# Sliding-window attention and a SMELU layer on one core: masks on VectorE, a new order of early loads and first-batch sessions, output quarters eight slots behind

## The chip, the cores and the metric

The kernel runs on one core of a Trainium2 chip. The metric is device time in microseconds for one execution; lower is better. The engines are TensorE (PE, with its weight loads as PEld), VectorE (DVE), ScalarE (ACT), GpSimd (POOL) and SyncE (SP, which only issues DMAs here).

## The reference

Eight batches of eight heads, 576 positions, head size 64. Attention looks at most 32 positions to each side. Its result, 4608 tokens by 512, goes through two weight matrices with a piecewise activation between them.

```python
scores = scale * np.matmul(q, k.transpose(0, 1, 3, 2))
mask = np.abs(pos[:, None] - pos[None, :]) <= window        # window = 32
attn = softmax(np.where(mask, scores, -1e9)); attn_out = np.matmul(attn, v)
x = attn_out.transpose(0, 2, 1, 3).reshape(B * S, H * D)    # 4608 x 512
h = x @ w_in                                                # 512 x 2048
g = np.where(h >= 1, h, np.where(h <= -1, 0.0, (h + 1) ** 2 / 4))
return g @ w_out                                            # 2048 x 512
```

## The kernel before, in words

All matmuls are in bf16. The order of the work on each engine is written out by hand (`manual_schedule`): an engine runs its instructions in the order in which the program issues them, and semaphores order engines against each other.

**The slots.** After a start-up part the main loop (L395) counts slots `a`. A slot works on token block t = a // 8 (256 tokens) and on f = a % 8 (256 of the 2048 hidden features). It issues eight matmuls of hp (L415, weights w_in, 256 columns each), on ScalarE rr = relu(0.5 h + 0.5) (L419), on VectorE mx = max(h, rr) (L422) and gT = min(rr, 1) * mx (L423). That product is the activation. The hp tiles come from two PSUM banks (pool ps_h); in slots 2, 3, 6, 7, 10, 11 they come from the output pool ps_o instead (L409). Of 144 slots, those whose predecessor issued a GpSimd mask (list `masked`, L392) write the max back into hp rather than into a tile of its own in SBUF (L421).

**Output.** From slot 14 on (LAG = 14) each slot also issues four matmuls with w_out (L438). Sixteen make one tile of 128 tokens by 512, in one of two banks of ps_o. ScalarE then copies it to osb (L442), of which there are three, and SyncE stores it. After the last hidden slot, 14 slots of output matmuls are left.

**Attention sessions.** A batch has five score sessions and five sum sessions. The table `ev` says which slot issues which (L368 to L381). A score session (L198; `scores8`, L226, for the last 96 positions) computes blocks of scores with 64 by 64 matmuls into a tile of two banks, applies exp on ScalarE to pt (L222, L240), and masks. In slots below PEM = 28 (`eng` is None, L397) TensorE adds a mask matrix to the scores ahead of the exp (`add_mask`, L191). From slot 28 on GpSimd multiplies pt by a mask of zeros and ones (L224, L242). A sum session (L246) multiplies pt with v and with ones, and its `end` computes 1 / sum on ScalarE as exp(-ln(sum)) (L280, L281). VectorE's product with it, which writes xT (L286, L289), is put off to the beginning of the next slot (`flush`, L404). A token block's hidden slots need the xT of all sums over its tokens.

**q and k.** For batches 0 to 2 they are loaded in halves (`load_long`), and TensorE transposes them in slots listed in L382 (`tpose`, L169). Two copies of each go to ScalarE before slot 15, and after that one to ScalarE and one to VectorE. Batches 3 to 7 are loaded whole (`load_nat`) and transposed by DMA from SyncE's queue.

**Queues.** All loads but the first four pieces of q are issued by GpSimd, in program order, on one queue; the tile framework lets eight be under way. The early ones stand in L116 to L155: q and k of batch 0's first half, v of batch 0, four pieces of w_in with 256 columns, then q and k of the second half mixed with the six larger pieces of w_in (`mix` puts one large load ahead of two small ones), batch 1's first half mixed with its v, w_out in quarters, and so on. Later loads are issued in slots fixed in L386 to L389; GpSimd's masks stand in the same queue.

Of the kernel before, what the change touches and what calls it, by code (L numbers as in the profile page):

```python
# [8 lines left out]
FP = mybir.dt.float32  # L9
# [6 lines left out]
def kernel(  # L16
# [19 lines left out]
    nc = tc.nc  # L36
# [67 lines left out]
    def load_w_in(c0, c1, h):  # L104
        nc.gpsimd.dma_start(out=w_in[64 * h:64 * h + 64, :, c0:c1],
                            in_=moe_w_in.rearrange("(h y d) f -> h d y f", h=2, d=64)[h][:, :, c0:c1])
# [25 lines left out]
    V.memset(ones, 1.0)  # L132
    for t in qTs:
        V.memset(t[:, 0:PAD], 0.0)
    for c in range(0, 512, 256):
        for h in range(2):
            load_w_in(c, c + 256, h)

    def mix(small, large):

        for n in range(0, max(len(small), 2 * len(large)), 2):
            for fn, *x in large[n // 2:n // 2 + 1] + small[n:n + 2]:
                fn(*x)
# [1 line left out]
    def halves(b, half):  # L145
        return [(load_long, b, half, t, y) for t in range(2) for y in range(NY)]

    mix(halves(0, 1), [(load_w_in, c, c + 512, h) for c in (512, 1024, 1536) for h in range(2)])
    mix(halves(1, 0), [(load_v, 1, n) for n in range(4)])
    load_w_out(0)  # L150
    load_w_out(1)
    mix(halves(1, 1), [(load_w_out, 2), (load_w_out, 3)])
    mix(halves(2, 0), [(load_v, 2, n) for n in range(4)])
    for fn, *x in halves(2, 1):
        fn(*x)  # L155


    kT = {}
# [29 lines left out]

    pt, pt8 = {}, {}

    def add_mask(ps, n, w):  # L191
        for a in range(2):
            for h in range(2):
                nc.tensor.matmul(ps[HD[a], h, :n * w].rearrange("p (n j) -> p n j", n=n), ident[HD[h], HD[h]],
                                 bias[HD[h], :w].rearrange("p (n j) -> p n j", n=1).to_broadcast([64, n, w]),
                                 start=True, stop=False, skip_group_check=True)

    def scores(b, ys, pars, cs, eng, pool=ps_s):  # L198

        if b not in pt:  # L200
            pt[b] = ptp.tile([128, 2, 2, 2, 512], BF, name="pt")
        ps = two_banks(pool)
        n = 0
        if eng is None:
            cols = (ys[1] - ys[0]) * (pars[1] - pars[0]) * (cs[1] - cs[0])
            add_mask(ps, cols, 128)
        for y1 in range(*ys):
            for par in range(*pars):
                for c2 in range(*cs):
                    c = 2 * c2 + par  # L210
                    for a in range(2):
                        for h in range(2):
                            s0 = S * (y1 + 2 * a) + 64 * c
                            nc.tensor.matmul(ps[HD[a], h, 128 * n:128 * n + 128], kT[b][HD[h], s0:s0 + 64],  # L214
                                             qTs[b % 3][HD[h], PAD + s0 - 32:PAD + s0 + 96],
                                             start=eng is not None, stop=True, skip_group_check=True)
                    n += 1
        p = pt[b][:, :, ys[0]:ys[1], pars[0]:pars[1], 128 * cs[0]:128 * cs[1]]
        m = 2 if n > cs[1] - cs[0] else 1
        p = p[:, :, ys[0] - ys[0]] if ys[1] - ys[0] == 1 else p[:, :, :, 0]  # L220
        like = "p h (y j) -> p h y j"
        A.activation(p, ps[:, :, :128 * n].rearrange(like, y=m), AF.Exp, scale=D ** -0.5)  # L222
        if eng is not None:
            eng.tensor_mul(p, p, mask4[:, :256 * n].rearrange("p (h j) -> p h j", h=2).rearrange(like, y=m))  # L224

    def scores8(b, eng, pool=ps_s):  # L226

        p = pt8[b] = ptp.tile([128, 2, 2, TAIL], BF, name="pt8")
        ps = two_banks(pool)
        if eng is None:  # L230
            add_mask(ps, 2, TAIL)
        for y1 in range(2):
            for a in range(2):
                for h in range(2):
                    s0 = S * (y1 + 2 * a) + MAIN
                    nc.tensor.matmul(ps[HD[a], h, TAIL * y1:TAIL * y1 + TAIL], kT[b][HD[h], s0 + 32:s0 + TAIL],
                                     qTs[b % 3][HD[h], PAD + s0:PAD + s0 + TAIL],
                                     start=eng is not None, stop=True, skip_group_check=True)
        p = p.rearrange("p h y j -> p h (y j)")
        A.activation(p, ps[:, :, :2 * TAIL], AF.Exp, scale=D ** -0.5)  # L240
        if eng is not None:
            eng.tensor_mul(p, p, mask8.rearrange("p (h j) -> p h j", h=2))  # L242

    muls = []

# [102 lines left out]

    NB = NT // TB
    NF = DFF // 256
    LAG = 14
    PEM = 28
    ev, tps = {}, {}

    def at(a, *todo):
# [7 lines left out]
                yield (sums, b, y1, lo, hi), (scores, b, (y1, y1 + 1), (0, 2), (2 * k, 2 * k + 2))  # L365
        yield (sums, b, 0, MAIN, S), (scores8, b)

    at(4, (scores, 0, (0, 1), (0, 2), (2, 4)), (scores8, 0, ps_n))  # L368
    at(5, (sums, 0, 0, TB, MAIN), (scores, 0, (1, 2), (0, 2), (2, 4)))
    at(6, (sums, 0, 1, TB, MAIN, ps_s), (sums, 0, 0, MAIN, S))  # L370
    seq = [x for b in range(1, B) for x in steps(b, 224)]
    at(12, seq[0][0])
    at(13, (*seq[1][0], ps_s))
    for n, a in enumerate((20, 22, 25, 27)):
        at(a, seq[2 + n][0])
    for n, a in enumerate((10, 11, 19, 20, 21, 26, 27)):
        at(a, seq[n][1])
    sl = [30, 32, 35, 39, 42, 45, 49, 52, 56, 59, 62, 65, 69, 73, 77, 81, 84, 88, 92]
    sl += [96, 99, 103, 106, 110, 113, 116, 120, 124, 128]
    for n, a in enumerate(sl):  # L380
        at(a, seq[6 + n][0], seq[7 + n][1] if n < len(sl) - 1 else None)  # L381
    for b, half, *a in ((0, 1, 1, 3), (1, 0, 8, 9), (1, 1, 17, 18), (2, 0, 23, 24), (2, 1, 28, 29)):  # L382
        for t in range(2):
            tps[a[t]] = [(b, 2 * half + part, t) for part in range(2)]
    loads, xps = {}, {}
    for b in range(LONG, B):  # L386
# [2 lines left out]
            loads.setdefault(a + t, []).append((b, t))  # L389
        for t in range(2):  # L390
            xps.setdefault(a + 9 + 2 * t, []).append((b, t))
    masked = [a for a in ev if a >= PEM and any(x[0] is not sums for x in ev[a])]  # L392

    gT = {}
    for a in range(NF * NB + LAG):  # L395
        t, f = divmod(a, NF)
        eng = None if a < PEM else P  # L397
        for b, x in loads.get(a, []):
            if x < 2:
                load_nat(b, x)  # L400
            else:
                for n in range(4):
                    load_v(b, n)
        flush()  # L404
        if t < NB:
            if f == 0:
                gT[t] = gtp.tile([128, 2 * NF, TB], BF, name="gT", tag="gT")
            r0 = TB * t % RING
            if a < LAG and a % 4 > 1:  # L409
                hp = ps_o.tile([128, 2, TB], FP, name="hp", tag="op")  # L410
            else:
                hp = ps_h.tile([128, 2, TB], FP, name="hp", tag="hp")
            for j in range(2):
                for n, kk in enumerate((0, 2, 1, 3)):
                    nc.tensor.matmul(hp[:, j], w_in[:, kk, 256 * f + 128 * j:256 * f + 128 * j + 128],  # L415
                                     xT[:, kk, r0:r0 + TB], start=n == 0, stop=n == 3)

            rr = ewp.tile([128, 2, TB], FP, name="rr")
            A.activation(rr, hp, AF.Relu, scale=0.5, bias=0.5)  # L419

            mx = hp if a - 1 in masked else ewp.tile([128, 2, TB], FP, name="mx")  # L421
            V.tensor_max(mx, hp, rr)  # L422
            V.scalar_tensor_tensor(gT[t][:, 2 * f:2 * f + 2], rr, 1.0, mx, op0=ALU.min, op1=ALU.mult)  # L423
        ends = []
        for fn, *x in ev.get(a, []):
            if fn is sums:
                ends.append(sums(*x))
            else:
                pool = (x.pop(),) if x[-1] in (ps_s, ps_n) else ()
                fn(*x, eng, *pool)  # L430
        for end in ends:
            end()
        if a >= LAG:
            for x in range(4 * (a - LAG), 4 * (a - LAG) + 4):
                tt, ff = divmod(x, 2 * NF)
                if ff == 0:
                    op = ps_o.tile([128, DM], FP, name="op", tag="op")
                nc.tensor.matmul(op, gT[tt // 2][:, ff, 128 * (tt % 2):128 * (tt % 2) + 128], w_out[:, ff],  # L438
                                 start=ff == 0, stop=ff == 2 * NF - 1)
                if ff == 2 * NF - 1:  # L440
                    osb = osp.tile([128, DM], FP, name="osb")
                    A.copy(osb, op)  # L442
                    nc.sync.dma_start(out=out[128 * tt:128 * tt + 128, :], in_=osb)
        if a in tps:
            copies = [tpose(b, n, t, (A.copy, V.tensor_copy)[i if a > LAG else 0], tp1((ps_s, ps_n)[i]))
                      for i, (b, n, t) in enumerate(tps[a])]
            for x in copies:
                x()
        for x in xps.get(a, []):
            xpose(*x)  # L450
# [30 lines left out]
```

The softmax here doesn't subtract the row's maximum and nothing guards it: scores larger than these inputs give would overflow.

## Time and profile before

| | us |
|---|---|
| median of 10 runs | 328.06 |
| lowest and highest | 327.46, 329.72 |
| profiled execution, its time | 327.81 |
| profiled execution, its span | 325.9 |

The page of the profile gives shares over the whole span. TensorE's matmul records overlap in time, since their ends are modelled, so the distance from one start to the next tells the pace. The costliest groups, mean duration of one instruction:

| group | count | mean, ns |
|---|---|---|
| L415 hidden matmul, 256 columns | 1152 | 275 (a record) |
| L438 output matmul, 512 columns | 576 | 380 (a record) |
| L419 ScalarE rr | 144 | 595 |
| L422 VectorE max into mx, into hp | 116, 28 | 690, 692 |
| L423 VectorE gT from mx, from hp | 116, 28 | 746, 687 |
| L224 GpSimd mask of 1024, L242 of 384 | 22, 6 | 2192, 911 |
| L222 ScalarE exp | 32 full | 1023 |
| L280, L281 Ln and Exp of 512 | 16, 16 | 593, 630 |

Row 2 of the page cuts the span into 40 slices of 8.15 us. The table of stretches, shown below in rows, gives: the stretch, then for PE, PEld, DVE, ACT and POOL the busy time with the number of instructions, then granted clock, DMA share and GB/s.

### The profile page before, as it was taken

The numbers are of one execution on the slowest core, as the hardware profiler recorded it, in microseconds if no ns is written. First come the engines' busy times: TensorE is split into PE (matmuls) and PEld (weight loads), VectorE is DVE, ScalarE is ACT, GpSimd is POOL, SyncE is SP. The second block draws the span as 40 slices with busy tenths as digits, with TensorE's granted clock in tenths as the row PEclk, the third lists the DMA queues.
The fourth block names the chain that finished last, engine by engine and source line by source line (L and its number), as shares of the span: only waits on it lengthen the run. The fifth ranks groups of instructions, "written<-read, shape, count | busy, mean of one in ns | idle before, by whom it ended". The sixth has DMA issues, their size and how long they took to land.

```text
span 325.9 us, 8581 instructions
## 1 busy us (share of the span) xinstructions
PE 310.7 (95%) x3667; PEld 203.3 (62%) x3667; DVE 233.6 (72%) x350; ACT 194.0 (60%) x319; POOL 139.8 (43%) x148
## 2 busy tenths in 40 slices
PE   8959799999999999999999999998999999999995
PEld 3536576666666666666666666666666666666642
DVE  2336888686778777878787877877797777877710
ACT  3637885767676655676555556666655766544411
POOL 8966639860234942486216922197212223000000
PEclk9978999999999999999999999999999999999999
DMA  9999999999759994999262996099931000001111
GB/s 144 130 175 164 155 204 149 139 165 110 103 73 143 86 156 108 123 95 142 68 143 45 149 177 126 34 89 164 154 89 36 34 34 33 34 32 61 38 66 64
DMA packets 121030, 34.54 MB, mean 106 GB/s; under 512 B 108704, under 2 KB 116128, under 8 KB 120992
## 3 DMA queue, kind: packets, MB, share of 16 engines
q0 software_dynamic: 92128, 18.06, 69.6%
q1 hardware_dynamic: 28864, 15.93, 19.8%
q8 instruction: 29, 0.48, 0.6%
q14 instruction: 9, 0.07, 0.1%
HBM read 36.70 MB, written 9.44 MB: 142 GB/s over the span
## 4 chain that ended last, share of the span: by engine, by line
PE 62%; POOL 15%; ACT 8%; issue 7%; DVE 4%; DMA 2%; ACTq 0%; POOLq 0%
PE hp L415 27%; PE op L438 26%; PE bb L274 5%; POOL pt L224 4%; POOL vn L101 4%; ACT pt L222 3%; POOL kn L93 2%; PE tp L179 2%; DMA qn<-in_q_dram 2%; ACT rr L419 2%; PE bb L214 2%; DVE gT L423 2%; POOL qn L93 2%; DVE hp L422 1%; ACT osb L442 1%
## 5 line engine op out<-in xcount | busy, mean ns | idle before, releaser
L415 PE MATMUL hp<-xT,w_in 128*128 128x256 bf16 x1152 | 151.1, 275 | 2.6 <-DVE gT L423 1.2
L438 PE MATMUL op<-w_out,gT 128*128 128x512 bf16 x576 | 145.9, 380 | 0.0
L419 ACT ACTIVATE rr<-hp 128x512 f32<-128x512 f32 x144 | 85.7, 595 | 92.0 <-PE hp L415 90.0
L415 PEld LDWEIGHTS <-w_in 128*128 128x128 bf16 x1152 | 111.1, 98 | 46.9 <-DVE gT L423 8.3
L422 DVE TENSOR_TENSOR mx<-hp,rr 128x512 f32<-128x512 f32 x116 | 80.0, 690 | 37.8 <-ACT rr L419 36.9
L423 DVE SCALAR_TENSOR_TENSOR gT<-rr,mx 128x512 bf16<-128x512 f32 x116 | 86.6, 746 | 4.0
L224 POOL TENSOR_TENSOR pt<-pt,mask 128x1024 bf16<-128x1024 bf16 x22 | 48.2, 2192 | 93.6 <-ACT pt L222 93.6
L438 PEld LDWEIGHTS <-gT 128*128 128x128 bf16 x576 | 53.4, 98 | 42.4
L222 ACT ACTIVATE pt<-bb 128x1024 bf16<-128x1024 f32 (+1 forms) x33 | 33.1, 1010 | 7.3 <-PE bb L214 6.0
L286 DVE TENSOR_TENSOR xT<-bb,rc 128x512 bf16<-128x512 f32 (+1 forms) x32 | 20.9, 654 | 23.1 <-ACT rc L281 23.1
L442 ACT COPY osb<-op 128x512 f32<-128x512 f32 x36 | 20.9, 581 | 15.2 <-PE op L438 14.8
L101 POOL DMA_DIRECT2D vn<-in_v_dram x32 | 27.6, 892 | 1.8 <-DMA w_in<-in_moe_w_in_dram 1.8
L281 ACT ACTIVATE rc<-lr 128x512 f32<-128x512 f32 (+2 forms) x40 | 23.5, 587 | 1.3
L274 PE MATMUL bb<-pt,ones 64*64 64x256 bf16 (+3 forms) x352 | 19.6, 255 | 3.4 <-POOL pt L224 1.2
L280 ACT ACTIVATE lr<-bb 128x512 f32<-128x512 f32 (+2 forms) x40 | 22.0, 550 | 0.4 <-PE bb L274 0.3
L422 DVE TENSOR_TENSOR hp<-hp,rr 128x512 f32<-128x512 f32 x28 | 19.4, 692 | 2.4 <-ACT rr L419 2.4
L423 DVE SCALAR_TENSOR_TENSOR gT<-rr,hp 128x512 bf16<-128x512 f32 x28 | 19.2, 687 | 1.0
L85 POOL DMA_DIRECT2D kn<-in_k_dram x24 | 13.1, 552 | 12.8 <-DMA w_out<-in_moe_w_out_dram 3.6
L274 PEld LDWEIGHTS <-ones 64*64 64x64 bf16 x352 | 11.0, 105 | 12.0 <-issue 10.7
L274 PE MATMUL bb<-pt,vn 64*64 64x128 bf16 (+3 forms) x712 | 18.4, 204 | 0.0
L274 PEld LDWEIGHTS <-vn 64*64 64x64 bf16 x712 | 16.8, 107 | 0.0
L242 POOL TENSOR_TENSOR pt<-pt,mask 128x384 bf16<-128x384 bf16 x6 | 5.5, 911 | 26.4 <-ACT pt L240 26.4
(44 smaller groups left out, 140.7 us busy)
## 6 DMA issues: line engine op xcount, KB each, us to landing
out_dram<-osb SPq DMA_DIRECT2D x36, 256.0 KB, 2.2
vn<-in_v_dram POOLq DMA_DIRECT2D x32, 144.0 KB, 8.0
qn<-in_q_dram POOLq DMA_DIRECT2D x10, 288.0 KB, 6.5
kn<-in_k_dram POOLq DMA_DIRECT2D x10, 288.0 KB, 8.2
w_out<-in_moe_w_out_dram POOLq DMA_DIRECT2D x4, 512.0 KB, 10.3
kn<-in_k_dram POOLq DMA_DIRECT2D x24, 72.0 KB, 4.6
w_in<-in_moe_w_in_dram POOLq DMA_DIRECT2D x6, 256.0 KB, 6.8
qn<-in_q_dram POOLq DMA_DIRECT2D x20, 72.0 KB, 6.2
```

Of the source, the lines that this page charges most:

```text
L101: nc.gpsimd.dma_start(out=vn[b][64 * a:64 * a + 64, :, h], in_=v[b, y:y + 2].rearrange("y s d -> (y s) d") .rearrange("(c r) d -> r c d", ...
L222: A.activation(p, ps[:, :, :128 * n].rearrange(like, y=m), AF.Exp, scale=D ** -0.5)
L224: eng.tensor_mul(p, p, mask4[:, :256 * n].rearrange("p (h j) -> p h j", h=2).rearrange(like, y=m))
L274: nc.tensor.matmul(bb[HD[h], a, o + c0:o + c1], ones[HD[a]] if c is None else vn[b][HD[a], c, h], p(a, h), start=n == 0, stop=True, skip_g ...
L280: A.activation(lr[:, :, :D0], bb[:, :, D0:2 * D0], AF.Ln)
L281: A.activation(rc[:, :, :D0], lr[:, :, :D0], AF.Exp, scale=-1.0)
L415: nc.tensor.matmul(hp[:, j], w_in[:, kk, 256 * f + 128 * j:256 * f + 128 * j + 128], xT[:, kk, r0:r0 + TB], start=n == 0, stop=n == 3)
L419: A.activation(rr, hp, AF.Relu, scale=0.5, bias=0.5)
L422: V.tensor_max(mx, hp, rr)
L423: V.scalar_tensor_tensor(gT[t][:, 2 * f:2 * f + 2], rr, 1.0, mx, op0=ALU.min, op1=ALU.mult)
L438: nc.tensor.matmul(op, gT[tt // 2][:, ff, 128 * (tt % 2):128 * (tt % 2) + 128], w_out[:, ff], start=ff == 0, stop=ff == 2 * NF - 1)
L442: A.copy(osb, op)
```

## The change

- Masks: `eng` is None only below slot 12, and VectorE from there on. GpSimd masks nothing. The mask is a function of its own, in one piece.
- The max always goes to a tile mx in SBUF; the list `masked` is gone.
- Output: work is cut into quarters of four matmuls of one output tile. Quarter x runs in slot x + 8 from slot 16 on; the first eight run in slots 11 to 15, as a table says (w_out's third quarter is used in slots 13 and 15, its fourth in slot 15). `pre` quarters stand ahead of the sessions, `post` ones after them. The order of a slot is otherwise kept.
- Early loads: the four small w_in pieces, all q pieces of the second half, one large w_in piece, all k pieces, the other five w_in pieces; then w_out's first quarter at the head of batch 1's first half, w_out's second and third quarter, v of batch 1, and the fourth quarter at the head of batch 1's second half.
- Batch 0's remaining sessions move two slots forward (slots 2 to 5), its k transposes to the end of slot 1. The `scores8` of batch 0 uses two banks of ps_o with an exp for each. Only slots 6 and 7 take hp from ps_o. Some sessions of batches 1 and 2 move by a slot or more.

```diff
-    for c in range(0, 512, 256):
-        for h in range(2):
-            load_w_in(c, c + 256, h)
...
-    mix(halves(0, 1), [(load_w_in, c, c + 512, h) for c in (512, 1024, 1536) for h in range(2)])
-    mix(halves(1, 0), [(load_v, 1, n) for n in range(4)])
-    load_w_out(0)
-    load_w_out(1)
-    mix(halves(1, 1), [(load_w_out, 2), (load_w_out, 3)])
+    w = [(load_w_in, c, c + d, h) for c, d in ((0, 256), (256, 256), (512, 512), (1024, 512), (1536, 512)) for h in range(2)]
+    x = halves(0, 1)
+    put(w[:4] + x[:4] + w[4:5] + x[4:] + w[5:])
+    mix(halves(1, 0), [(load_w_out, 0)])
+    put([(load_w_out, 1), (load_w_out, 2)] + [(load_v, 1, n) for n in range(4)])
+    mix(halves(1, 1), [(load_w_out, 3)])
...
+    def mask(eng, p, m):
+        if eng is not None:
+            eng.tensor_mul(p, p, m)
...
-        if eng is not None:
-            eng.tensor_mul(p, p, mask4[:, :256 * n].rearrange("p (h j) -> p h j", h=2).rearrange(like, y=m))
+        mask(eng, p, mask4[:, :256 * n].rearrange("p (h j) -> p h j", h=2).rearrange(like, y=m))
...
-        A.activation(p, ps[:, :, :2 * TAIL], AF.Exp, scale=D ** -0.5)
+        if pool:
+            for h in range(2):
+                A.activation(p[:, h].rearrange("p y j -> p (y j)"), ps[h], AF.Exp, scale=D ** -0.5)
+        else:
+            A.activation(p.rearrange(like), bb[:, :, :2 * TAIL], AF.Exp, scale=D ** -0.5)
+        mask(eng, p, mask8.rearrange("p (h y j) -> p h y j", h=2, y=2))
...
-    LAG = 14
-    PEM = 28
+    quarters = {11: ([], [0]), 12: ([], [1]), 13: ([], [2]), 14: ([], [4, 5]), 15: ([6], [3, 7])}
...
-    at(4, (scores, 0, (0, 1), (0, 2), (2, 4)), (scores8, 0, ps_n))
-    at(5, (sums, 0, 0, TB, MAIN), (scores, 0, (1, 2), (0, 2), (2, 4)))
-    at(6, (sums, 0, 1, TB, MAIN, ps_s), (sums, 0, 0, MAIN, S))
+    at(2, (scores, 0, (0, 1), (0, 2), (2, 4)), (scores8, 0, ps_o))
+    at(3, (sums, 0, 0, TB, MAIN), (scores, 0, (1, 2), (0, 2), (2, 4)))
+    at(4, (sums, 0, 1, TB, MAIN, ps_s))
+    at(5, (sums, 0, 0, MAIN, S))
...
-    at(12, seq[0][0])
-    at(13, (*seq[1][0], ps_s))
-    for n, a in enumerate((20, 22, 25, 27)):
+    at(15, seq[0][0], (*seq[1][0], ps_s))
+    for n, a in enumerate((20, 22, 23, 27)):
         at(a, seq[2 + n][0])
-    for n, a in enumerate((10, 11, 19, 20, 21, 26, 27)):
+    for n, a in enumerate((11, 12, 19, 20, 22, 26, 27)):
         at(a, seq[n][1])
...
-    for b, half, *a in ((0, 1, 1, 3), (1, 0, 8, 9), (1, 1, 17, 18), (2, 0, 23, 24), (2, 1, 28, 29)):
+    for b, half, *a in ((0, 1, 1, 1.5), (1, 0, 9, 10), (1, 1, 17, 18), (2, 0, 24, 25), (2, 1, 28, 29)):
...
-    masked = [a for a in ev if a >= PEM and any(x[0] is not sums for x in ev[a])]
...
+    def quarter(x):
+
+        tt, ff = divmod(x, 4)
+        if tt not in op:
+            op[tt] = ps_o.tile([128, DM], FP, name="op", tag="op"), []
+        o, done = op[tt]
+        for j in range(4 * ff, 4 * ff + 4):
+            nc.tensor.matmul(o, gT[tt // 2][:, j, 128 * (tt % 2):128 * (tt % 2) + 128], w_out[:, j],
+                             start=not done, stop=len(done) == 2 * NF - 1, skip_group_check=True)
+            done.append(j)
...
-    for a in range(NF * NB + LAG):
+    for a in range(NF * NB + NF):
         t, f = divmod(a, NF)
-        eng = None if a < PEM else P
+        eng = None if a < 12 else V
+        pre, post = quarters.get(a, ([], [a - NF] if a >= 2 * NF else []))
...
-            if a < LAG and a % 4 > 1:
+            if a in (6, 7):
                 hp = ps_o.tile([128, 2, TB], FP, name="hp", tag="op")
...
-            mx = hp if a - 1 in masked else ewp.tile([128, 2, TB], FP, name="mx")
+            mx = ewp.tile([128, 2, TB], FP, name="mx")
...
-        if a >= LAG:
-            for x in range(4 * (a - LAG), 4 * (a - LAG) + 4):
...
+        for x in post:
+            quarter(x)
```

## The prediction

> **What bounds the kernel now.** I read the page first (busy shares, the clock row), then the table of stretches, then TensorE's rows in order of time, from which I took where each slot begins (a slot is one pass of the loop over `a`: eight hidden matmuls, and later four output matmuls), and last the waits and the rows of one attention session.
>
> ```profile
> PE 310.7 (95%) x3667; PEld 203.3 (62%) x3667; DVE 233.6 (72%) x350; ACT 194.0 (60%) x319; POOL 139.8 (43%) x148
> ...
> PEclk9978999999999999999999999999999999999999
> ```
> ```profile
> 83.80:282.00 198.20, 195.39 (x2326) 130.12 (x2323) 157.18 (x225) 124.45 (x208) 86.57 (x60) 1.00 0.87 100
> ```
> ```profile
> 290.00:310.00 20.00, 20.00 (x138) 13.33 (x137) 15.74 (x24) 8.90 (x15) 0.00 (x0) 1.00 0.11 40
> 310.00:326.00 16.00, 11.94 (x56) 5.20 (x54) 1.09 (x2) 2.34 (x4) 0.00 (x0) 1.00 0.18 67
> ```
> TensorE sets the time. In 290 to 310 us it has no gap, and there the slots begin 1.74 us apart: 0.87 for eight hidden matmuls, 0.86 for four output matmuls (0.216 each). The last row is the end: after the last hidden group (307.96) 60 output matmuls run alone, 12.9 us, then 4.2 us for the last copy and store. From 83.8 to 282 VectorE is busy 157.2 of 198.2 us (79%), so it has room, but little. Slot starts divide the span: slot 0 at 14.8, slot 8 at 36.2, slot 14 (first output matmuls) at 46.0, slot 16 at 49.48, slot 30 at 83.81, slot 143 at 307.96.
>
> ```profile
> 20.83 1.17 PE L179 MATMUL tp<-ident,qn 128*64 128x128 bf16 x18 [3.75 <-DMA qn<-in_q_dram]
> ```
> ```profile
> PEld L415 <- DVE gT L423: 8.3, 21, 0.8
> ...
> PE bb L274 <- POOL pt L224: 1.2, 3, 0.9
> ```
> ```profile
> 156.73 0.40 PE L214 MATMUL bb<-qT,kT 64*64 64x128 bf16 x16
> ...
> 157.18 1.02 ACT L222 ACTIVATE pt<-bb 128x1024 bf16<-128x1024 f32 x1 [0.21 <-PE bb L214]
> 157.72 0.69 DVE L423 SCALAR_TENSOR_TENSOR gT<-rr,mx 128x512 bf16<-128x512 f32 x1
> ...
> 158.28 2.13 POOL L224 TENSOR_TENSOR pt<-pt,mask 128x1024 bf16<-128x1024 bf16 x1 [3.99 <-ACT pt L222]
> ...
> 159.26 0.57 ACT L442 COPY osb<-op 128x512 f32<-128x512 f32 x1
> 159.38 0.69 DVE L286 TENSOR_TENSOR xT<-bb,rc 128x512 bf16<-128x512 f32 x1 [0.97 <-ACT rc L281]
> ...
> 160.36 0.70 DVE L422 TENSOR_TENSOR hp<-hp,rr 128x512 f32<-128x512 f32 x1 [0.28 <-ACT rr L419]
> ...
> 161.09 0.69 DVE L423 SCALAR_TENSOR_TENSOR gT<-rr,hp 128x512 bf16<-128x512 f32 x1
> ...
> 161.84 1.05 PE L415 MATMUL hp<-xT,w_in 128*128 128x256 bf16 x8 [0.27 <-DVE gT L423]
> ```
> What to see: GpSimd's mask (2.13) waits for the exp and almost nobody waits for the mask. VectorE idles 0.97 us in the session, between the gT of 157.72 and the xT of 159.38. And the slot after a session writes its max back into hp, so its PSUM bank is held until the gT of 161.09 ends: the hidden matmuls of slot 68 begin at 161.84 instead of 161.41 (end of the four output matmuls begun at 160.54).
>
> [...] of the 116 gT instructions that read rr and mx from SBUF, the 24 that overlap a GpSimd mask take 0.955 us on average, the other 92 take 0.692. [...] after the idle 3.75 us at 17 to 20.8 us the sixteen hidden matmuls from 21.93 take 3.60 us, twice the normal.
>
> **The change part by part.** Sum against the profiled span, 325.9 us.
>
> *Steady part, slots 30 to 143 (before: 224.15 us).* 22 full and 6 small masks leave GpSimd and go to VectorE. Cost there: 22 x 0.69 + 6 x 0.36 = 17.3 us of VectorE time; back come 24 x (0.955 - 0.687) = 6.4 us of contention. VectorE then is at 168 of about 194 us, 87%. On the path it costs nothing while the idle time before xT covers it: those waits are 0.56 to 1.30 us, mostly over 0.7. In the session above the exp ends at 158.20, gT at 158.41, the mask would run 158.41 to 159.10, and xT starts at 159.38 as before. Queued behind the mask are that xT and the next slot's max, which frees the hp bank; there 0.35 us of slack is left (max ends 161.06, TensorE needs the bank at 161.41). [...]
> What goes: the in-place max. Its stalls, read as slots over 1.74 us with no attention in them, are at slots 47, 51, 67, 75, 79, 83, 115 (0.28 to 0.43) and 34, 86, 105, 122 (0.05): 2.6 us. Of waits for GpSimd masks, slots 45, 62 and 99 exceed their like by 0.26, 0.24, 0.94: 1.4 us; next in line there is the mask on VectorE, done two slots earlier than needed. Sum -4.0: 220.1 us. The store copy moves from slots with a%4==1 to a%4==3 with the new lag, so it meets other sessions (35, 39, 59, 99, 103): nothing, since the bank is now free at the max.
>
> *End.* The lag goes from 14 to 8 slots: after slot 143 come 36 output matmuls instead of 60, 24 x 0.216 = 5.2 us less; 17.98 becomes 12.8. This is moved, not saved: the 24 matmuls now stand before slot 16.
>
> *Slots 0 to 15 (before: 49.48 us at slot 16).* Loads are one after another on GpSimd's queue. By landing events a q or k piece takes about 0.37 us, a 256-column w_in piece 0.66, a 512-column one about 1.6 (1.26 to 2.4), v 1.4, w_out 2.6. The new order puts all q pieces behind the four small w_in (landed 15.6): q at about 17.1 (before 20.7), then one w_in and k at about 20.6, both w_in for slot 2 at 22.2, all w_in at 28.8 as before (same bytes), w_out 0 at 31.4, 1 at 37, 2 at 39.6, v 45, w_out 3 at 47.8. TensorE: q transposes at 17.3, an idle 2.6 us, k transposes to 21.3, slot 2 at 22.2, scores in slots 2 and 3, sums in 3 to 5. Then ScalarE's chain (rr 0.60, exp 1.02, Ln and Exp 1.1 per session) puts the last xT of batch 0 at 32.9, and slot 8, which needs it, at 33.0 (before 36.2). Slots 8 to 10 go at VectorE's and ScalarE's pace as before (5.1 us from slot 8 to 11): slot 11 at 38.1. Slots 11 to 15: 5 hidden groups 4.4, eight quarters 6.9, scores 1.0, two sums 1.2, small waits 0.3: 13.8, slot 16 at 51.9. Quarters 3 and 7 run at 50.2, after w_out 3; quarter 2 at 43.9, after w_out 2. So 2.4 later than before with 5.2 us more work done.
>
> *Slots 16 to 29 (before: 34.33 us).* 14 x 1.736 = 24.3; six transposes 6 x 0.73 = 4.4; scores alone 0.3 and 0.4, sums with scores 0.9, 0.77, 0.82, small sums 0.59. VectorE masks replace the mask matmuls of six sessions (24 matmuls; about 0.25 us of TensorE a session, slot 26's 0.67 against 0.35 to 0.4). Against that, slots 20, 23 and 27 use a mask made one slot earlier: in slot 19 the exp ends at 59.02 and gT at 59.31, the mask ends about 60.0, and TensorE would want it at 59.6: 0.4 each for 20 and 27, 0.1 for 23; two waits for k copies 0.6. Together 34.2.
>
> *GpSimd's queue* keeps only loads, so those of batches 3 and 4 go as soon as a buffer is free. They meet the output stores (one took 5.5 us under load, 64.56 to 70.06); three osb buffers at one store in 4 slots give over 20 us, so I cost it at nothing; without that cover the copy of osb would hold an output bank and TensorE.
>
> Sum: 51.9 + 34.2 + 220.1 + 12.8 = 319.0, which is 6.9 less than 325.9. The profiled execution took 327.81, 1.9 more than its span, and the median is 0.25 above that: 321.2.
>
> **Rivals.**
> (1) The early part gains nothing: k or w_in come later, or the idle wait for k halves the clock, and slot 8 stays at 36.2. For it: the clock row[...]. Against: q comes first and all w_in at the same time. +3.2: 324.4.
> (2) The stalls in the steady part aren't the in-place max's but the pile of ScalarE work, and stay: +4.0, 325.2. Against: the bank is released 0.7 us earlier.
> (3) Slower: VectorE becomes the bound. [...] the next max is late, then the hp bank, then TensorE: +11.2, 332.4. It decides from 0.25 us a session on (7 us). [...]
> (4) Better than summed: w_in and v land earlier and slots 11 to 15 lose no wait: slot 16 at 49, 318.
>
> **How the numbers follow.** A measurement here can tell about 0.2% (0.66 us) from no change. Forecast case (318.5 to 323): 0.52. Rival 1: 0.20. Rival 2: 0.08. Rival 4 and below: 0.08. Rival 3: 0.08. Early loss and stalls together (about 328, no change): 0.04. Faster 0.88, same 0.04, slower 0.08. The range 316.5 to 326.5 leaves out the last two and little else.
>
> **What would show it.** Right: slot 16 near 52 us, 36 output matmuls after the last hidden group, VectorE masks of 0.69, gT at 0.69 throughout, steady slots without attention all at 1.74, no TensorE wait on gT. Wrong: [...] hidden matmuls that wait for max, a half clock beyond 26 us, slot 16 after 55.

## The result, and the profile after

The changed kernel takes 324.38 us (median of 9 runs, 323.69 to 325.86); the kernel before takes 328.18 (median of 32). The ratio is 0.989 (95%: 0.9873 to 0.9906): 3.8 us faster, where the forecast was 6.9 and the predicted time 321.2. The profiled execution took 323.97 us, with a span of 322.2. Of the experiments' executions one with a lag of 14 and one with three buffers ran over 1.5% slower than the fastest of their kernel, at a lower clock, and are left out of the medians. Cut at the slot starts that the prediction used, from TensorE's rows, in us:

| stretch | before | forecast | after |
|---|---|---|---|
| start of slot 8 | 36.2 | 33.0 | 34.58 |
| start of slot 11 | 41.3 | 38.1 | 39.42 |
| start of slot 16 | 49.48 | 51.9 | 53.02 |
| slots 16 to 29 | 34.33 | 34.2 | 35.43 |
| slots 30 to 142 | 224.15 | 220.1 | 221.01 |
| slot 143 to the end | 17.98 | 12.8 | 12.74 |
| span | 325.9 | 319.0 | 322.2 |

The forecast misses the span by 3.2 us: 1.1 before slot 16, 1.2 in slots 16 to 29, 0.9 in the steady part.

The page of the kernel after: busy shares and the clock row.

```profile
PE 306.4 (95%) x3643; PEld 202.2 (63%) x3643; DVE 246.5 (77%) x384; ACT 194.3 (60%) x320; POOL 86.4 (27%) x120
...
PEclk9998999999999999999999999999999999999999
```

The row of the table of stretches for the steady part (the same 198.2 us length as in the row of before):

```profile
88.40:286.60 198.20, 197.03 (x2373) 132.84 (x2368) 169.42 (x258) 127.18 (x212) 24.77 (x24) 1.00 0.84 96
```

TensorE still sets the time. VectorE has 169.4 us of work in the stretch instead of 157.2 (the forecast said 168), and GpSimd only issues loads.

One steady session of the kernel after, in order of time, to be set against the session of before:

```profile
160.12 0.40 PE L218 MATMUL bb<-qT,kT 64*64 64x128 bf16 x16
...
160.57 1.02 ACT L226 ACTIVATE pt<-bb 128x1024 bf16<-128x1024 f32 x1 [0.21 <-PE bb L218]
161.11 0.69 DVE L448 SCALAR_TENSOR_TENSOR gT<-rr,mx 128x512 bf16<-128x512 f32 x1
...
161.72 0.68 DVE L193 TENSOR_TENSOR pt<-pt,mask 128x1024 bf16<-128x1024 bf16 x1
...
162.78 0.69 DVE L296 TENSOR_TENSOR xT<-bb,rc 128x512 bf16<-128x512 f32 x1 [0.37 <-ACT rc L291]
163.06 1.04 PE L441 MATMUL hp<-xT,w_in 128*128 128x256 bf16 x8
163.38 0.68 DVE L447 TENSOR_TENSOR mx<-hp,rr 128x512 f32<-128x512 f32 x1
```

The mask is where the prediction put it: on VectorE, 0.68 us, between gT and xT. Over the whole trace the masks of 1024 take 0.684 us on average and those of 384 take 0.351; the 0.69 and 0.36 of the sum were not shown by the trace of before, which has no VectorE mask. xT still waits 0.37 us for ScalarE's rc, so the mask is on no path here. The max goes to mx, and no TensorE group waits for a gT any more.

The start, TensorE's rows of the kernel after:

```profile
17.24 0.69 PE L179 MATMUL tp<-ident,qn 128*64 128x128 bf16 x18
21.60 0.69 PE L179 MATMUL tp<-ident,kn 128*64 128x128 bf16 x18 [3.67 <-DMA kn<-in_k_dram]
22.97 1.87 PE L441 MATMUL hp<-xT,w_in 128*128 128x256 bf16 x8 [0.68 <-DMA w_in<-in_moe_w_in_dram]
```

The wait for k is 3.67 us and not 2.6; q landed at 16.99 as forecast, k at 21.46 where 20.6 was forecast. After it the clock records give half speed from 22.7 to 26.1, and the hidden group of slot 2 takes 1.87 us instead of about 1.04.

The end: the last 36 output matmuls, then the last copy of an output tile.

```profile
310.34 7.93 PE L412 MATMUL op<-w_out,gT 128*128 128x512 bf16 x36
...
318.31 0.58 ACT L417 COPY osb<-op 128x512 f32<-128x512 f32 x1 [2.87 <-PE op L412]
```

Two places in between were in nobody's list. The first is slot 16:

```profile
52.23 0.62 DVE L296 TENSOR_TENSOR xT<-bb,rc 128x448 bf16<-128x448 f32 x1 [0.46 <-ACT rc L291]
53.02 0.38 PE L441 MATMUL hp<-xT,w_in 128*128 128x256 bf16 x2
53.41 0.62 DVE L296 TENSOR_TENSOR xT<-bb,rc 128x448 bf16<-128x448 f32 x1 [0.56 <-ACT rc L291]
54.09 0.81 PE L441 MATMUL hp<-xT,w_in 128*128 128x256 bf16 x6 [0.68 <-DVE xT L296]
```

Both sum sessions of batch 1 stand in slot 15. ScalarE makes their Ln and Exp one after the other (0.54 and 0.58 us each, from 51.05 and from 52.23), the second xT ends at 54.03, and slot 16, the first of the new batch, needs it after two matmuls.

The second is slot 73. The rows are those of SyncE's queue (SPq, stores and DMA transposes of q and k) and of GpSimd's loads (POOL), then TensorE's:

```profile
158.27 2.92 SPq L186 DMA_TRANSPOSE qT<-qn  x1
...
165.10 2.45 POOL L93 DMA_DIRECT2D qn<-in_q_dram  x2 [19.10 <-DMA qT<-qn]
165.61 0.33 SPq L418 DMA_DIRECT2D out_dram<-osb  x1
...
166.11 4.82 SPq L186 DMA_TRANSPOSE kT<-kn  x1
```
```profile
176.48 0.42 PE L218 MATMUL bb<-qT,kT 64*64 64x128 bf16 x16 [0.79 <-DMA kT<-kn]
```

Batch 5's q transpose, once landed (164.56), frees the q buffer; GpSimd, which has no masks to do and stood 19.1 us at this wait, loads batch 6's q at once. Batch 5's k transpose is queued behind an output store on SyncE, starts beside that load and lands at 176.44: 10.3 us, where the median of the k transposes before is 4.7. The scores of slot 73 want it at 175.7. In the kernel before, the same q load started at 176.39, since GpSimd's masks held its queue.

### The profile page after: what moved, and what is told of

Read it like the earlier page. It is cut to its first block, busy times and chain, and to the rows that moved or that the text cites. A ratio compares the mean times of both kernels' runs of the same rounds, so it can differ in the third digit from the quotient of the medians.

```text
span 322.2 us, 8537 instructions
## 1 busy us (share of the span) xinstructions
PE 306.4 (95%) x3643; PEld 202.2 (63%) x3643; DVE 246.5 (77%) x384; ACT 194.3 (60%) x320; POOL 86.4 (27%) x120
## 4 chain that ended last, share of the span: by engine, by line
PE 80%; DMA 7%; DVE 5%; ACT 3%; POOL 3%; issue 1%; POOLq 0%; ACTq 0%
PE op L412 36%; PE hp L441 34%; PE bb L284 5%; DMA w_in<-in_moe_w_in_dram 3%; DMA kT<-kn 3%; PE bb L218 2%; DVE mx L447 2%; DVE gT L448 1%; POOL kn L85 1%; POOL vn L101 1%; PE tp L179 1%; DVE xT L296 1%; ACT lr L290 1%; ACT rc L291 1%; ACT pt L226 1%
## 5 line engine op out<-in xcount | busy, mean ns | idle before, releaser
L447 DVE TENSOR_TENSOR mx<-hp,rr 128x512 f32<-128x512 f32 x144 | 99.2, 689 | 42.2 <-ACT rr L445 40.0
L448 DVE SCALAR_TENSOR_TENSOR gT<-rr,mx 128x512 bf16<-128x512 f32 x144 | 99.6, 692 | 4.9
L417 ACT COPY osb<-op 128x512 f32<-128x512 f32 x36 | 20.8, 581 | 11.6 <-PE op L412 11.2
L93 POOL DMA_DIRECT2D qn<-in_q_dram x10 | 12.3, 1244 | 56.7 <-DMA qT<-qn 56.7
L193 DVE TENSOR_TENSOR pt<-pt,mask 128x1024 bf16<-128x1024 bf16 (+1 forms) x34 | 20.9, 616 | 0.8 <-ACT pt L226 0.8
L85 POOL DMA_DIRECT2D kn<-in_k_dram x24 | 13.0, 555 | 10.5 <-issue 3.3
L93 POOL DMA_DIRECT2D kn<-in_k_dram x10 | 12.1, 1225 | 12.8 <-DMA kT<-kn 11.5
L218 PE MATMUL bb<-qT,kT 64*64 64x128 bf16 x520 | 13.5, 220 | 1.6 <-DMA kT<-kn 0.8
```

The costliest lines, as they stand in the source:

```text
L93: nc.gpsimd.dma_start(out=x[:, :, h], in_=src[b, NY * h:NY * h + NY].rearrange("y s d -> (y s) d") .rearrange("(u p) d -> p u d", p=128))
```

## The experiments

All are edits of the kernel after. Times are medians, ratios are to the kernel before; "steady" is slots 30 to 142.

**Masks back on GpSimd** from slot 28.

```diff
-        eng = None if a < 12 else V
+        eng = None if a < 12 else V if a < 28 else P
```

> The changed kernel with one thing undone: from slot 28 on GpSimd multiplies the masks again (max still in its own tile). Theory (the moved masks themselves are worth little; TensorE lost 1.4 us to late GpSimd masks before, and gT slowed by contention is off the path): gT overlapping a GpSimd mask near 0.95 us again, two or three late-mask waits of 0.2 to 0.9 us, while the wait for the k transpose at slot 73 (0.98 us) goes because the masks pace the loads again. Against the changed kernel 0 to +1.5 us: 324.4 to 326. Rival (masks on VectorE cost TensorE time): faster than the changed kernel by 1 us or more.

Measured: 326.17 us, ratio 0.9935 (0.9913 to 0.9956). Steady 222.89, 1.88 more than after. Late masks cost 0.24, 0.24 and 0.92 at slots 45, 62 and 99, as in the kernel before (1.4 in all), and the wait of slot 73 (0.98) is gone: both expected. Not expected: slots 47 and 64 lose 0.73 each.

```profile
117.97 2.20 POOL L193 TENSOR_TENSOR pt<-pt,mask 128x1024 bf16<-128x1024 bf16 x1
118.13 2.60 DVE L448 SCALAR_TENSOR_TENSOR gT<-rr,mx 128x512 bf16<-128x512 f32 x1
...
122.69 2.14 DVE L448 SCALAR_TENSOR_TENSOR gT<-rr,mx 128x512 bf16<-128x512 f32 x1
...
126.01 0.38 PE L441 MATMUL hp<-xT,w_in 128*128 128x256 bf16 x2 [0.57 <-DVE mx L447]
```

A gT that reads rr and mx from SBUF and begins just after the start of a GpSimd mask takes 2.14 to 2.60 us instead of 0.69; the xT and the max behind the gT of 122.69 are late, their bank stays held, and TensorE waits at slot 47. The gT of 118.13 ends at 120.73, 0.56 us after the mask (120.17). The others are like it: in this trace and that of the kernel before, all 27 gT instructions that read rr and mx and begin inside a mask end 0.55 or 0.56 us after it, and the 30 inside which a mask begins keep their 0.69. In the kernel before the longest gT was 1.73, and the gT after a session read hp from PSUM and took 0.687, inside a mask too (seven of them). So no mask slowed a gT behind an in-place max there: the two edits, masks off GpSimd and max into mx, belong together.

**Max in place again**, in the slot after a masking session.

```diff
+    masked = [a for a in ev if a >= 28 and any(x[0] is not sums for x in ev[a])]
...
-            mx = ewp.tile([128, 2, TB], FP, name="mx")
+            mx = hp if a - 1 in masked else ewp.tile([128, 2, TB], FP, name="mx")
```

> The changed kernel with one thing undone: in slots after a masked session the max is again written over hp, so its bank is held until gT ends; masks stay on VectorE. Theory (the in-place max caused the steady stalls): stalls of 0.3 to 0.4 us reappear two slots after sessions that share a slot with the store copy, now 35, 39, 59, 99 and 103, none at 45, 65, 73, 77, 81: +1.5 to +2.5 us, 326 to 327. Rival (the pile of ScalarE work made them, not the bank): no change, 324.4.

Measured: 326.21 us, ratio 0.9954 (0.993 to 0.9979). Steady 222.94, 1.93 more than after. Stalls at slots 41 (0.21), 61 (0.32), 101 (0.32), 105 (0.43), two slots after the sessions 39, 59, 99 and 103, in whose slots a store copy falls since the lag is 8, and 0.05 or 0.06 at 34, 51, 67, 86, 122: 1.5 us. The session 35, also expected, made none at 37. Another 0.28 of the 1.93 is not the max's: the wait of slot 73 for its k transpose is that much longer in this trace. VectorE's and TensorE's rows at slot 41:

```profile
114.05 0.69 DVE L449 SCALAR_TENSOR_TENSOR gT<-rr,hp 128x512 bf16<-128x512 f32 x1
114.66 0.68 DVE L448 TENSOR_TENSOR mx<-hp,rr 128x512 f32<-128x512 f32 x1
114.80 1.05 PE L442 MATMUL hp<-xT,w_in 128*128 128x256 bf16 x8
```

The group of 114.80 starts when the gT that reads hp is done (114.74); the output matmuls ahead of it ended about 114.58. The stalls moved with the store copy, as the theory said. ScalarE's pile makes rr late, but the same pile stands in the kernel after and stalls nothing there, so the rival, that ScalarE alone makes the stalls, is rejected.

**Lag of 14 again**: no output matmul before slot 14.

```diff
-    for a in range(NF * NB + NF):
+    for a in range(NF * NB + 14):
...
-        pre, post = quarters.get(a, ([], [a - NF] if a >= 2 * NF else []))
+        pre, post = [], [a - 14] if a >= 14 else []
```

> The changed kernel with the output lag of before: quarter x in slot x + 14, so two instead of eight quarters stand ahead of slot 16 and 14 instead of 8 after the last hidden slot. Theory (work moved, not saved: slots 13 to 15 are TensorE-bound and pay for the early quarters in full; only the quarters of slots 11 and 12 fill waits): slot 16 starts 4.2 to 5.2 us earlier and the end is 5.2 us longer: 0 to +1 us, 324.4 to 325.4. Rival (the shorter end is a gain of its own): +5 us, 329.5.

Measured: 325.61 us, ratio 0.9923 (0.9895 to 0.9951). The end is 17.97 again (5.23 more), but slots 8 to 15 take 15.28 us, only 3.16 less than after's 18.44, where 24 matmuls fewer are 5.18. So 2.0 us of those matmuls ran in waits. Neither side had this: 1.9 us by the rows from slot 8 on, 1.2 by the medians. Against the kernel before, nothing was filled (slots 11 to 15: 8.18 before, 13.60 after, 5.42 more for 5.18 of matmuls): the waits are those of the new session order. In the rows of this run 1.06 us of them stand at the end of slot 15, where the sums are piled, and 0.36 in slots 12 and 13, for VectorE's max; in the kernel after the quarters cover both. The collision of slot 73 is not gone but elsewhere: with this lag it is batch 4's k transpose that starts after a load and takes 11.2 us, and slot 56 loses 1.18.

**Each VectorE mask issued twice** (ones and zeros: pt is the same after the second).

```diff
-            eng.tensor_mul(p, p, m)
+            for _ in range(2):
+                eng.tensor_mul(p, p, m)
```

> The changed kernel with every VectorE mask issued twice (zeros and ones, so pt is the same), which doubles the disputed cost: 0.69 us more in each full session, 0.35 in each small one, 17 us of VectorE time in the steady part. Theory (one mask fits in VectorE's idle time before the xT of about 1 us, the second overruns it by some 0.4 us, and 0.35 us of slack to the hp bank takes most of that): +1 to +5 us, 325.5 to 329.5, with hidden matmuls that wait for max. Rival (VectorE is already the bound): +15 us or more, 340.

Measured: 326.82 us, ratio 0.997 (0.9956 to 0.9984). The row of its steady part:

```profile
90.70:289.00 198.30, 197.04 (x2373) 132.83 (x2368) 182.12 (x285) 127.10 (x212) 24.73 (x24) 1.00 0.75 94
```

VectorE does 12.7 us more in this stretch, 92% of it, and TensorE's pace is the same: steady 221.20, 0.19 more than after. What the second mask costs, 2.0 us, is all in slots 16 to 29 (37.46), where sums follow one slot after the mask. The total lies in the expected range, but my expectation of steady stalls was wrong; VectorE, busy for 85% of this stretch in the kernel after, is much farther from being the bound than I had held. Rival 3's 11.2 us rested on the author's assumption of a slower mask, which no run shows; even two masks, 1.36 us a session, bring only the 0.19 in this part.

**The early loads in the old order**, the sessions left in their new slots.

```diff
-    x = halves(0, 1)
-    put(w[:4] + x[:4] + w[4:5] + x[4:] + w[5:])
-    mix(halves(1, 0), [(load_w_out, 0)])
-    put([(load_w_out, 1), (load_w_out, 2)] + [(load_v, 1, n) for n in range(4)])
-    mix(halves(1, 1), [(load_w_out, 3)])
+    put(w[:4])
+    mix(halves(0, 1), w[4:])
+    mix(halves(1, 0), [(load_v, 1, n) for n in range(4)])
+    load_w_out(0)
+    load_w_out(1)
+    mix(halves(1, 1), [(load_w_out, 2), (load_w_out, 3)])
```

> The changed kernel with the early loads in the order of before (w_in mixed with q and k, v of batch 1 ahead of w_out). Theory (slot 2 and with it ScalarE's chain to slot 8 hang on the k pieces, which land at 21.5 now and at about 25.5 in the old order; w_out's quarters come at 40.5 to 49): slot 8 some 3 to 4 us later, slot 16 as much or, through w_out, more: +3 to +5 us, 327.5 to 329.5. Rival (ScalarE's chain sets slot 8 whatever the loads do): under +1 us.

Measured: 328.45 us, ratio 1.0001 (0.9982 to 1.002). TensorE waits 3.99 us for q and 3.51 for k, the clock is at half for 10.24 us (3.41 after), slot 2 starts at 27.05 and slot 8 at 39.05; from slot 16 on all stretches are those of after within 0.21. The load order, the longer half clock included, is worth 4 us with the sessions in their new slots. Whether it would gain as much with the sessions in their old slots was not run; the sessions that were moved two slots forward do need it, since with the old loads slot 8 starts 2.8 us later than in the kernel before.

**The k transposes one slot after the q transposes** on SyncE's queue, not two.

```diff
-            xps.setdefault(a + 9 + 2 * t, []).append((b, t))
+            xps.setdefault(a + 9 + t, []).append((b, t))
```

> The changed kernel with each k transpose by DMA one slot after the q transpose instead of two, so that for batch 5 it stands ahead of an output store on SyncE's queue. Theory (the k transpose of batch 5 is late because it stands behind the store, and is then slowed by a load that the q transpose has let go): the 0.98 us wait at slot 73 goes, 323.4. Rival (the load alone slows it): most of the wait stays.

Measured: 323.62 us, ratio 0.9851 (0.9825 to 0.9876). The k transpose of batch 5 now starts right behind the q transpose (162.08), before the load (166.24). It lands at 167.50, after 5.4 us, slot 73 waits for nothing, and steady is 220.03: 0.98 less than after.

**A third buffer for q and k**, so that the load need not wait for the transpose.

```diff
-        x = dst[b] = nat.tile([128, NU, 2, D], BF, name=nm, tag=nm)
+        x = dst[b] = nat.tile([128, NU, 2, D], BF, name=nm, tag=nm, bufs=3)
```

> The changed kernel with three buffers instead of two for the q and k of batches 3 to 7, so that no load waits for a transpose just then; the order on SyncE's queue is kept. Theory (a load set free by the q transpose of batch 5 doubles the time of the k transpose, 10.3 us from issue to landing instead of 4.7): without it the transpose lands by 171 to 172 us and slot 73 doesn't wait: 323.4. Rival (the place behind the store is enough): the wait of 0.98 us stays, 324.4.

Measured: 325.63 us, ratio 0.9926 (0.9894 to 0.9958). SyncE's queue in two places:

```profile
168.07 2.81 SPq L186 DMA_TRANSPOSE kT<-kn  x1
```
```profile
95.62 7.12 SPq L186 DMA_TRANSPOSE qT<-qn  x1
102.92 5.35 SPq L186 DMA_TRANSPOSE kT<-kn  x1
```

Behind the same store, but with no load beside it, the k transpose of batch 5 lands after 4.6 us, and slot 73 doesn't wait. So the place in the queue alone isn't the cause: here the transpose took 4.6 us with no load beside it and 10.3 behind one, and the place decides whether it meets one. It also matters which starts first. In the kernel after, batch 3's k transpose also had a load beside it, which started 2.0 us later, and landed after 6.0 us:

```profile
97.91 2.77 SPq L186 DMA_TRANSPOSE kT<-kn  x1
```
```profile
99.91 2.43 POOL L93 DMA_DIRECT2D qn<-in_q_dram  x2 [16.24 <-DMA qT<-qn]
```

The buffer only moves the collision: batch 3's q transpose now starts behind loads, its issue alone takes 7.12 us, the transposes land after 12.8 and 7.4 us, and slot 39 loses 0.88, of which 0.69 is the wait for kT. Steady 220.91, nothing won.

**All k pieces before the large w_in**, batch 0's sessions one slot earlier.

```diff
-    put(w[:4] + x[:4] + w[4:5] + x[4:] + w[5:])
+    put(w[:4] + x + w[4:])
...
-    at(2, (scores, 0, (0, 1), (0, 2), (2, 4)), (scores8, 0, ps_o))
+    at(1, (scores, 0, (0, 1), (0, 2), (2, 4)), (scores8, 0, ps_o))
...
+        if a == 1:
+            transposes(a)
```

> A further step: all k pieces ahead of the large w_in pieces, and batch 0's remaining sessions one slot earlier still, with the first scores ahead of slot 2's hidden matmuls. Theory (the early part hangs on k and on ScalarE's chain from the k copies to the last xT of batch 0): k lands near 18.5, slot 8 starts 2 to 3.5 us earlier, slot 16 is then held by w_out's last quarter (48.4) and starts 1.5 to 3 us earlier: 321.5 to 323. Rival (w_in holds slots 2 to 7, so nothing is won): 324.4.

Measured: 324.75 us, ratio 0.9899 (0.9878 to 0.992). k lands at 19.46 and slot 8 starts at 33.79, but slot 11 at 40.97 and slot 16 at 54.88, later than after. TensorE's row in slot 10:

```profile
38.37 1.57 PE L448 MATMUL hp<-xT,w_in 128*128 128x256 bf16 x8 [2.05 <-DVE mx L454]
```

From 29.5 to 40 us VectorE runs without a gap, at the end max and gT alone, 1.33 us a slot, and TensorE waits for it; after that the clock is halved a second time, from 38.7 to 42.1. The theory failed: k wasn't the limit beyond slot 8.

**Sessions spread**: the first sum session of batch 1 from slot 15 to 14, the small score session from 22 to 21, with the k transposes of above.

```diff
-    at(15, seq[0][0], (*seq[1][0], ps_s))
+    at(14, seq[0][0])
+    at(15, (*seq[1][0], ps_s))
...
-    for n, a in enumerate((11, 12, 19, 20, 22, 26, 27)):
+    for n, a in enumerate((11, 12, 19, 20, 21, 26, 27)):
```

> The k transpose one slot after q (known: the wait at slot 73 goes) and two sessions moved: the first sum session of batch 1 from slot 15 to 14, the small score session of batch 1 from slot 22 to 21. Theory (the part from slot 16 to 29 lost 2 us to sessions that lie too close: slot 16 waits 0.85 for an xT made in slot 15, slot 23 waits 0.64 for a mask made in slot 22): both waits go, that part takes 34 us or less instead of 35.4; against the version with the transpose alone -1 to -1.5 us, 322.2 to 322.7. Rival (the waits are ScalarE's total work and only move): no change, 323.6.

Measured: 322.64 us, ratio 0.9819 (0.9783 to 0.9854). Slot 16's excess falls from 0.85 to 0.09, slots 16 to 29 take 34.60 instead of 35.43. Slots 8 to 15 take 0.24 more, so the net is 0.6. The small score session brought hardly 0.1: slot 23 still waits 0.32 for an xT.

**Two large w_in pieces ahead of q**, batch 0's transposes in slot 3 instead of 1 and its sessions a slot later; and **this with the sessions spread** and the k transposes of above.

```diff
-    put(w[:4] + x[:4] + w[4:5] + x[4:] + w[5:])
+    put(w[:6] + x + w[6:])
...
-    at(2, (scores, 0, (0, 1), (0, 2), (2, 4)), (scores8, 0, ps_o))
+    at(3, (scores, 0, (0, 1), (0, 2), (2, 4)), (scores8, 0, ps_o))
...
+        if a == 3:
+            transposes(a)
```

> The changed kernel with the first two large w_in pieces ahead of q and k, and slots 2 and 3 ahead of batch 0's transposes, its sessions in slots 3 to 6. Theory (from slot 4 to 10 VectorE's 1.4 us a slot is the bound, since slots 2 to 7 all come late; two hidden slots done while q and k are still on their way take 2.8 us of it off[...]): slot 8 near 33.5 to 34.5, slot 11 1 to 2 us earlier than 39.4, slot 16 1 to 2 us earlier: 322.4 to 323.6. Rival (the chain from k to the last xT of batch 0 alone sets slot 11): 324.4.

> The last two and the k transpose together. Theory: gains add where they lie in different parts: 320.5 to 322. Rival (w_out's last quarter, landed at 48.4, holds slot 15 whatever comes before, so that the early gain is lost): 322.5.

Measured: 325.33 us, ratio 0.9903 (0.9869 to 0.9938), and 324.03, ratio 0.9865 (0.9831 to 0.99). Slot 2 starts early (20.41 and 19.87), slot 8 late (36.27 and 36.88): k comes later, and the chain from k to the last xT of batch 0 sets slot 8. In the first run the theory failed and the rival came nearer; in the second neither did, since the loss lay before slot 16 (from there on its stretches are those of the spread run). With k_first it brackets the case: k earlier runs into VectorE, k later into its own chain.

**Sessions spread, and the wait for k filled**: twelve 512-column matmuls on a tile of zeros, whose result nobody uses, between the q and the k transposes of slot 1.

```diff
+            if part == 1.5:
+                keep_warm(12, ps_h, "hp")
```

> The version with spread sessions and the early k transpose, plus twelve matmuls on a tile of zeros, whose result is not used, in TensorE's wait for k in slot 1 (3.67 us in the changed kernel). Theory (that wait halves TensorE's clock for 3.4 or 6.8 us, and the longer interval alone moved slot 8 by 1.5 us between runs whose first 28 slots are the same program): the clock is not halved, slot 8 starts 0.7 to 2 us earlier than 35.4, and the times scatter less: 320.8 to 322.2. Rival (slots 2 to 8 hang on loads and ScalarE, so the clock costs nothing): 322.6.

Measured: 321.09 us (320.72 to 321.38), ratio 0.9769 (0.9738 to 0.98): faster than both kernels. TensorE's rows:

```profile
17.74 2.76 PE L318 MATMUL z<-warm 128*128 128x512 bf16 x12
21.23 0.69 PE L179 MATMUL tp<-ident,kn 128*64 128x128 bf16 x18 [0.73 <-DMA kn<-in_k_dram]
22.47 1.03 PE L442 MATMUL hp<-xT,w_in 128*128 128x256 bf16 x8 [0.55 <-DMA w_in<-in_moe_w_in_dram]
```

Slot 2's group takes 1.03 us instead of 1.87, and the clock records show full speed up to 318.8 us. Slot 8 starts at 32.88, slot 16 at 51.56, and the span is 318.95. The theory held: k landed at 21.09, as in the run with the sessions spread alone (21.11), where the clock was at half for 6.83 us and slot 8 started at 35.41. That is 2.5 us, more than the 0.7 to 2 expected.

## Why the prediction was right or wrong

The measured 324.38 us lies in the stated range, but beyond the forecast case (318.5 to 323), and the gain is 3.8 us of the 6.9.

**The end: right.** 12.74 for 12.8.

**The steady part: right in mechanism, one term missing.** The stalls of the in-place max and the waits for late masks are gone, and each comes back when its edit is undone: 1.5 us of stalls, 1.4 us of late masks (with 1.46 of slow gT, and without the 0.98 of slot 73). VectorE's masks cost TensorE nothing, and the margin is larger than I gave it: "there 0.35 us of slack is left" is true of that slot, yet 12.7 us more of VectorE work cost 0.19. Chance 0.08 for rival 3 was too much. The step that failed is "GpSimd's queue keeps only loads, so those of batches 3 and 4 go as soon as a buffer is free ... so I cost it at nothing". I set those loads only against the output stores. They cross the DMA transposes of q and k on SyncE's queue, a user that the sum left out: 0.98 us at slot 73, shown by the runs that undo it from different sides.

**Slots 16 to 29: wrong.** Forecast 34.2, measured 35.43. I priced each session by its work and the masks by when they end, but not two sum sessions in one slot ahead of the slot that needs both xT: 0.85 at slot 16, which shrinks to 0.09 when one of them is moved. At slot 23 I gave 0.1 for a late mask; the wait is 0.64 and is for the xT that stands behind that mask. The sum has a slip besides: its terms add to 34.0, not 34.2.

**Slots 0 to 15: direction right, 1.1 too early.** All of it is there at slot 8 (34.58 for 33.0); from 8 to 16 the sum was 18.9 and the measured 18.44. The term was the idle wait for k, "an idle 2.6 us", which measured 3.67, with the half clock that follows; when that wait is filled slot 8 starts at 32.88, though k lands at 21.09, still later than the 20.6 of the sum. So the half clock, which the sum left out, is most of the 1.6 us at slot 8. Rival 1 named this and its sign, and its total, 324.4, is the measured time; but its cause carries only a third of the miss: slot 8 did gain 1.65 of the 3.2 us. That the total agrees is a coincidence. The half clock beyond 26 us, one of the signs of being wrong, came (to 26.1), but it tells little: in the kernel before it lasts to 26.6.

**"This is moved, not saved"** holds against the kernel before, but without those matmuls the new order would have had 2 us of waits.

When the three faults are taken out, in the last run, the stretches are slot 16 at 51.56 (51.9), then 34.60 (34.2), 220.03 (220.1) and 12.75 (12.8), a span of 318.95 against the 319.0 of the sum. The sum priced most of the work rightly and missed what the new order makes wait. That it agrees to 0.05 is in part luck, since 0.4 too little in slots 16 to 29 meets 0.3 too much before slot 16.

**The scatter between executions** goes in part with the clock. The mean clock and the time of ten single executions of the kernel after go together: seven at 0.995 took 323.7 to 325.2 us, three at 0.987 to 0.989 took 325.3 to 325.9. In the traces the half clock lasts 3.41 us or 6.83 (10.24 with the old loads). Two kernels that are the same up to slot 28 show the price: slot 2 starts at 23.23 and 23.28, slot 8 at 34.50 with masks on GpSimd (3.41) and at 36.05 with the max in place (6.83). The longer lengths are two and three times the shortest. So kernels that wait for k differ by up to 1.5 us without an edit, and I draw differences of that size from the stretches of the traces, not from medians.

What went with one length or two can be read from the table of stretches, cut at the clock records. The kernel after, ahead of the half clock and in it, then max_in_place, the two halves of its half clock:

```profile
19.27:22.69 3.42, 0.69 (x18) 0.56 (x18) 0.57 (x1) 0.58 (x1) 2.43 (x4) 1.00 1.18 185
22.69:26.11 3.42, 3.14 (x41) 2.03 (x42) 0.61 (x1) 1.58 (x4) 1.71 (x4) 0.50 1.17 175
```
```profile
22.11:25.52 3.41, 2.33 (x20) 1.23 (x20) 0.00 (x0) 1.59 (x3) 1.86 (x4) 0.50 1.05 149
25.52:28.93 3.41, 3.41 (x64) 2.50 (x60) 1.38 (x2) 2.29 (x5) 0.83 (x2) 0.50 1.18 189
```

TensorE was busy for 3.14 us of the first 3.41 in the one and for 2.33 in the other, where it stood idle a second time. The kernel before had a half clock of two such lengths as well, with 2.39 us busy in the first and 3.32 in the second. In all 13 traces in which a half clock begins between 19 and 26 us it ended after the first length of 3.41 us in which TensorE was busy for 92% or more, and went on after every one with 70% or less. In the 3.41 us ahead of it TensorE was not idle throughout: it was busy for 20% of them in the kernel after (0.69 us) and in the kernel before (0.68 us), and for 41% (1.38 us) in mask_twice. No run shows where a limit lies, or whether the busy share sets it: 59% was followed by a half clock in all_three, 49% there was not.

What stays open: why a DMA transpose that starts behind GpSimd's loads is slower, in the issue (7.12 us) as well as in the landing (12.8 us). No run here shows the cause of either, nor why transposes that meet no load differ (4.6 to 6.7 us).

## What to carry to other kernels

Before you take work off an engine that also issues DMAs, ask what that work was pacing: its loads can start earlier (here batch 6's q at 165.10 instead of 176.39), and the transfers on the other queues are candidates for the collision, transposes as much as stores (10.3 us instead of 4.7); here it was enough to put the transpose ahead of the load (5.4 us). Price a slot by who needs its results next, not only by its work: two sessions with one consumer cost more than their sum (0.85 us at slot 16). When TensorE must wait some 3 us for a load, a dozen matmuls on nothing can be worth more than another order of the loads (2.5 us at slot 8, where k_first and w_in_two_more_first won nothing in the time).

## What the runs showed of the hardware

- Of the 140 DMA transposes of q or k in the traces, the 118 that start with no load of GpSimd's queue under way land after 4.6 to 6.7 us, even where a load starts beside them (28 of these). The nine that start behind loads which last 3.9 us or more after that take 7.4 to 13.3 us, and their issue on SyncE 4.7 to 7.1 us instead of 2.6 to 3.6.
- After waits of TensorE for loads at 17 to 25 us the half clock lasted 3.41, 6.83 or 10.24 us in these traces. It ended with the first 3.41 us of it in which TensorE was busy for 92% or more; in max_in_place TensorE stood idle for 1.08 of the first 3.41 us, and it lasted 6.83. With twelve matmuls in the first wait (spread_filled) the trace has no half clock there, and the six executions lie within 0.66 us.
- A VectorE gT with two inputs in SBUF that begins inside a GpSimd mask ends 0.55 or 0.56 us after the mask and so takes up to 2.60 us instead of 0.69; one that begins before the mask keeps 0.69, and with one input in PSUM it kept 0.687 inside a mask too (seven in the kernel before).
